# Batching half-array products and pulling a product ahead of its pair in a TensorE-bound mLSTM, Fourier-mix and MLP kernel

## The chip, the cores and the metric

The kernel runs on one core of a Trainium2 chip. Its time is the device time in microseconds (us). Runs of one kernel spread by about ±0.3 to ±0.5% (the kernel before: 420.44 to 422.69 us in the rounds of pair_only, 420.89 to 424.94 in those of best4), so differences below one per cent are given with a 95% interval from rounds (five for each experiment) in which the kernel in question and the kernel before ran on the same chip. A program on one core has no second die to be compared with; all runs used here count as fast. What does differ between runs is the mean clock granted to TensorE (0.991 to 1.000 in the runs of the changed kernel), which each run records, and which will matter.

In line numbers the kernel before and the changed one differ: L837 of the kernel before is L847 of the changed one (products of the first batch's MLP), L749 is L759, L897 is L907 (full-array products of the later MLPs), L902 is L912 (their 64-row products), L906 is L916 (adds), L772 is L782, L785 to L795 are L795 to L805, and the weight sum L971 is L998 (L988 in pair_only and pair_late). Lines up to L550 are the same in both.

## The reference, cut to what matters

```python
# four batches, 8 heads, 768 positions, head size 40
for t in range(S):                                  # attention, by decayed sums
    C = f_stab * C + i_stab * outer(v[t], k[t]); n = f_stab * n + i_stab * k[t]
    y[t] = sigmoid(o_gate[t]) * (C @ q[t]) / max(abs(n @ q[t]), 1)
x = heads side by side                              # 768 x 320
u = x + real(fft2(x))                               # Fourier mix
un = layernorm(u)
out = u + relu(un @ w_ch1) @ w_ch2                  # MLP, 320 -> 1280 -> 320
```

## The kernel before: the parts that matter

The kernel works through each batch in chunks of 128 positions. While TensorE does the MLP of one batch, the attention chunks of the next batch are woven in. Every piece of work is put into a plan under a slot and a phase, and emitted in that order:

```python
EVAC, FILL, MAIN, FILL_PE = range(4)          # phases within a slot
def at(slot, phase, fn, *args):
    plan.setdefault((slot, phase), []).append((fn, args))
```

An attention chunk has products of three shapes: the scores `ps` (L465) use half of the array's rows (40*128 in the trace, two at a time, 7 ns apart), the state product `ph<-qg,C` (L479) is full, and the chunk products `ph<-W,kvt` (L486) and `pc` (L496) use half of its columns (128*41 and 128*40, in pairs as well). The plan of a chunk, cut:

```python
def plan_mlstm(b, s0, stride=3):
    for c in range(NT):
        s = s0 + stride * c
        ...
        at(s - 1 if last else s, FILL_PE + (2.05 if last else 2), mlstm_scores, b, c)   # TensorE
        if b > 0:
            at(s + 1, FILL, mlstm_mask, b, c)                                           # GpSimd L443
        at(... s + 1, FILL + 0.1, mlstm_scale_q, b, c)                                  # GpSimd L431, qg
        at(s + 2, FILL, mlstm_decay, b, c)                                              # GpSimd L455
        at(... s + 2, FILL, mlstm_weigh, b, c)                                          # VectorE L471
        at(... s + 3, FILL_PE, mlstm_from_state, b, c)                                  # TensorE L479
        at(... s + 3, FILL_PE + 3, mlstm_from_chunk, b, c)                              # TensorE L486
        at(s + 3, FILL_PE + 3, mlstm_to_state, b, c)                                    # TensorE L496, VectorE L513/L515
        at(... s + 4, FILL, mlstm_gather, b, c)                                         # ScalarE L524, GpSimd L526
        ...
        at(x, FILL + 0.05, mlstm_finish, b, c)                                          # VectorE L544 to L550
```

The MLP has 320 = 128 + 64 + 128 features, so it too has products on half the rows (`tails`). From the second batch on, two groups of columns are multiplied by a scheme with sums in place of one of the products, one pair of hidden blocks at a time; `p1` is used four times, with copies and adds between:

```python
elif step == 2:
    product(p3, block(w1x["S4"], i), mlp_u(1, 2), True)
    product(p1, block(w1x["S3"], i), T3)
    nc.scalar.copy(out=h22, in_=p1)
else:
    tails(1, (p3, p5)); tails(0, (p2, p1))       # 64-row products
    product(p1, A[1, 1], T4)
    add(h12, p3); add(h22, p5); add(h11, p2)     # VectorE
    nc.scalar.activation(out=h21, in_=p1, func=AF.Relu, scale=-1.0)
```

During the first batch's MLP the weights, which come as 64-bit words, are unpacked on the side: `take` is two VectorE steps (L344, L346) that start a piece, `convert` is ScalarE's, `join` three more of VectorE (L358, L360, L364). And between an MLP's halves stands the inverse square root of the layer norm, four VectorE steps and twelve small GpSimd steps:

```python
when += [((s, 0.7), (s + 1, 0.7), (s + 2, 0.6)) for s in (33, 36, 39, 42, 45)]   # take, convert, join
...
at(s_mlp + NFF, FILL + 0.6, mix_rstd, b)
at((56, 57, 58, 72)[n], FILL + 0.4, out_weight_sums, n)                          # VectorE L971 (L988 in pair_only)
```

Of the kernel before, what the change touches and what calls it, by code (L numbers as in the profile page):

```python
# [19 lines left out]
L = 128  # L20
NT = S // L
# [5 lines left out]
NFF = DFF // L  # L27
TAIL = DM - 2 * L
TG = NT // 2
# [21 lines left out]
def kernel(  # L51
# [14 lines left out]
    nc = tc.nc  # L66
# [18 lines left out]
    def bank(name, shape, n=None):  # L85

        return ps_m.tile(shape, FP, name=name, tag=f"pm{next(turn) if n is None else n}")
# [16 lines left out]
    w1_sb = const.tile([L, 2, DFF], FP, name="w1_sb")  # L104
# [17 lines left out]
    def at(slot, phase, fn, *args):  # L122
        plan.setdefault((slot, phase), []).append((fn, args))
# [7 lines left out]
    EVAC, FILL, MAIN, FILL_PE = range(4)  # L131
# [405 lines left out]
    def mlstm_finish(b, c):  # L537

        k = chunks.pop((b, c))
        if c == 0:  # L540
# [9 lines left out]
        nc.vector.tensor_tensor(out=xs[b][:, c, 0:DM].rearrange("p (h d) -> p h d", d=D), in0=h1[:, :, 0:D], in1=sc,  # L550
                                op=OP.mult)

    def plan_mlstm(b, s0, stride=3):
        for c in range(NT):
            s = s0 + stride * c
            if b > 0:
                t = 22 + 2 * c if b == 1 and c < 3 else s - 5
                at(t, FILL, mlstm_load, b, c)
                at(t, FILL, mlstm_load_max, b, c)
                at(t, FILL, mlstm_load_decay, b, c)  # L560
                at(s, FILL, mlstm_load_o, b, c)
            if (b, c) > (0, 0):
                at(s, FILL, mlstm_exp, b, c, 0)
                at(s + 1, FILL - 0.5, mlstm_exp, b, c, NP)
                last = (b, c) == (0, NT - 1)
                at(s - 1 if last else s, FILL_PE + (2.05 if last else 2), mlstm_scores, b, c)
                if b > 0:
                    at(s + 1, FILL, mlstm_mask, b, c)
            at(s, FILL, mlstm_scale_v, b, c)
            at(s if (b, c) == (0, 2) else s + 1, FILL + 0.1, mlstm_scale_q, b, c)  # L570
            at(s + 2, FILL, mlstm_decay, b, c)
            end = (b, c) == (0, NT - 1)
            at(s + 1 if end else s + 2, FILL - 0.4 if end else FILL, mlstm_weigh, b, c)
            at(s + 2 if end else s + 3, FILL_PE, mlstm_from_state, b, c)
            at(s + 2 if end else s + 3, FILL_PE + (2 if end else 3), mlstm_from_chunk, b, c)
            at(s + 3, FILL_PE + 3, mlstm_to_state, b, c)
            at(s + 3 if end else s + 4, FILL, mlstm_gather, b, c)
            if b == 0:
                t, x = ((8, 11), (11, 14), (13, 14), (14, 15.5), (17, 18), (18, 21))[c]
            else:  # L580
                t = s + (8, 8, 7, 5, 5, 5)[c]
                x = t + 1
            at(t, FILL_PE + ((2.5 if c < 4 else 1) if b == 0 else 1), mlstm_turn, b, c, b == 0 and c < 4)
            at(x, FILL + 0.05, mlstm_finish, b, c)


# [259 lines left out]
    def hidden(gr, f):  # L846
        return hid[gr, f % 2][:, f // 2 * TG * L:(f // 2 + 1) * TG * L]  # L847
# [7 lines left out]
    def block(t, n):  # L855
        return t[:, n * L:(n + 1) * L]
# [20 lines left out]
    def mlp_u(gr, ch):  # L877
        return uT_bufs[gr][:, ch].rearrange("p c t -> p (c t)")
# [8 lines left out]
    def mlp_block(b, i, step):  # L887



        k = mixes[b]
        f = 2 * i
        T2, T3, T4 = w1x["T"]
        A = {(r, ch): block(w1_sb[:, ch], f + r) for r in range(2) for ch in range(2)}

        def product(bank, w, u, start=False):
            nc.tensor.matmul(bank, w, u, start=start, stop=True, skip_group_check=True)  # L897

        def tails(gr, banks):
            for r, bank in enumerate(banks):  # L900
                rows = slice(r * TAIL, (r + 1) * TAIL)
                nc.tensor.matmul(bank, block(w1t_sb, i)[rows], mlp_u(gr, 1)[rows], start=False, stop=True,  # L902
                                 skip_group_check=True)

        def add(h, bank):
            nc.vector.tensor_tensor(out=h, in0=h, in1=bank, op=OP.add)  # L906

        if step == 0:
            k.pm = [bank("pm", [L, TG * L], n) for n in (range(4) if i % 2 else range(3, -1, -1))]
        p1, p2, p5, p3 = k.pm  # L910
        (h11, h21), (h12, h22) = ([hidden(gr, f + r) for r in range(2)] for gr in range(2))
        if step == 0:  # L912
            product(p1, A[0, 0], mlp_u(0, 0), True)
            product(p2, A[0, 1], mlp_u(0, 2), True)
            nc.scalar.copy(out=h11, in_=p1)
        elif step == 1:  # L916
            product(p5, A[1, 0], mlp_u(1, 0), True)
            product(p1, block(w1x["S2"], i), T2)
            nc.scalar.copy(out=h12, in_=p1)  # L919
            add(h12, p5)  # L920
        elif step == 2:
            product(p3, block(w1x["S4"], i), mlp_u(1, 2), True)
            product(p1, block(w1x["S3"], i), T3)
            nc.scalar.copy(out=h22, in_=p1)
        else:
            tails(1, (p3, p5))
            tails(0, (p2, p1))
            product(p1, A[1, 1], T4)
            add(h12, p3)
            add(h22, p5)  # L930
            add(h11, p2)
            nc.scalar.activation(out=h21, in_=p1, func=AF.Relu, scale=-1.0)

    def mlp_relu_in_place(gr, f):
# [95 lines left out]
    def plan_mlp(b, s):  # L1030
        groups = range(NT // TG)
        for i in range(NFF // 2) if b > 0 else ():
            for step in range(4):
                at(s, MAIN, mlp_block, b, i, step)
                s += 1
            end = i == NFF // 2 - 1
            for n, (gr, f) in enumerate(((1, 2 * i + 1), (1, 2 * i), (0, 2 * i))):
                at(*((s, EVAC) if end else (s + n, MAIN + 0.5)), mlp_relu_in_place, gr, f)
        for gr in groups if b == 0 else ():
            for f in range(NFF):  # L1040
                at(s, MAIN, mlp_in, b, gr, f)
                s += 1
                if f % 2:
                    at(s, EVAC, mlp_relu, b, gr, f - 1)
                    at(s, EVAC, mlp_relu, b, gr, f)
        if b > 0:
            for j in range(1, 5):
                at(s - (5, 4, 3, 3)[j - 1], FILL_PE + 0.3, hidden_sums, 0, (j,), 0, NFF // 2 - 2)
            at(s, EVAC, hidden_sums, 0, (1, 2), NFF // 2 - 2, NFF // 2)
            at(s, MAIN + 0.1, hidden_sums, 0, (3, 4), NFF // 2 - 2, NFF // 2)  # L1050
        for n in range(TG) if b > 0 else ():
            for step in range(4):
                at(s, MAIN, mlp_out_pair, b, n, step)
                if n < TG - 1 and step > 1:
                    for j in (2 * step - 3, 2 * step - 2):
                        at(s, MAIN + 0.6, hidden_sums, n + 1, (j,))
                s += 1
        for gr in groups if b == 0 else ():
            for i in range(TG):
                for half in range(2):  # L1060
                    at(s, MAIN, mlp_out, b, gr, i, half)
                    s += 1
                at(s, EVAC, mlp_store, b, gr, i)
# [6 lines left out]
    def plan_batch(b, s_mlstm, s_mix, s_mlp):  # L1070
        plan_mlstm(b, s_mlstm)
        done = [s_mlstm + 3 * (j + NT // 2) + 7 for j in range(NT // 2)]
        assert s_mix >= done[-1] and s_mlp >= s_mix + 9
        late = [s_mlp + 2 * c for c in range(TG)]
        if b == 0:
            feat = [s_mix + 1, s_mix + 1, s_mlp + 3]
            turn = [s_mix + 2, s_mix + 3, s_mix + 4]
            add = turn + [s_mlp, s_mlp + 4, s_mlp + 6]
            late = [s_mlp + 2, s_mlp + 5, s_mlp + 7]
        else:  # L1080
            feat = [s_mix + c for c in ((3, 4, 6) if b == 1 else (3, 4, 7))]
            add = [s_mix + c for c in ((4, 4, 5, 6, 7, 7) if b == 1 else (4, 4, 5, 6, 8, 9))]
            turn = [s_mix + c for c in ((5, 6, 6) if b == 1 else (6, 7, 8))]
            late = [s_mix + c for c in ((7, 8, 8) if b == 1 else (9, 10, 10))]
            at(s_mlp, EVAC + 0.5, mlp_sums)
        plan_mix(b, s_mix, done, feat, add, turn + late)
        at(s_mlp + NFF, FILL + 0.6, mix_rstd, b)
        plan_mlp(b, s_mlp)
# [143 lines left out]
```

## Time and profile before

| kernel before | |
|---|---|
| time, median of the first three runs | 421.74 us (421.09 to 422.83) |
| span of the profiled run | 419.2 us |
| TensorE busy | 408.1 us, 97% |
| mean granted clock | 0.999 |

A reader should take three things from it. TensorE is the bound, so only its own stream counts. The stream has gaps of two kinds: small ones at each change of array shape (0.13 to 0.2 us each, with the late pass behind them; last section), and waits. And the waits are few; of the eleven lines in the view of TensorE's waits, these four are the ones to compare later (columns: what waited and for what; us in total, times, longest):

```profile
PE ph L479 <- DVE den L544: 0.6, 1, 0.6
PE po L999 <- DVE x L949: 0.6, 2, 0.3
PE pm L837 <- DVE x L749: 0.5, 1, 0.5
...
PE ph L479 <- POOL qg L431: 0.2, 1, 0.2
```

There is nearly nothing to be removed here. Everything that the change moves on VectorE and GpSimd must stay within that slack.

### The profile page before, as it was taken

To read this page: it belongs to the slowest core of one execution; us is meant where nothing else is said; L and a number is where in the kernel's file an instruction comes from. 1 tells how busy PE (TensorE), PEld (TensorE's weight loads), DVE (VectorE), ACT (ScalarE), POOL (GpSimd) and SP (SyncE) were. 2 spreads that over 40 slices of the span, in tenths; PEclk is the share of its full clock that TensorE was granted. 3 is DMA by queue.
4 is the path that set the end of the run, shared out by engine and by line. 5 is a ranking of instruction groups with operands and counts; after the bars stand their busy time and mean duration, and the time that the engine had idled before them with its cause. 6 is when DMAs were issued, how large, how long until landed. Compare 5 with 4: busy or idle time off the path is not lost.

```text
span 419.2 us, 8001 instructions
## 1 busy us (share of the span) xinstructions
PE 408.1 (97%) x2966; PEld 302.4 (72%) x2966; DVE 288.8 (69%) x682; ACT 189.5 (45%) x493; POOL 112.9 (27%) x194
## 2 busy tenths in 40 slices
PE   8999999999999999999999999999999999999997
PEld 6877555566567778776549998976559988455996
DVE  8789895777895638777765569788663786335652
ACT  6986376686561222654455413744451113355000
POOL 5554201468431520442231430351220000020000
PEclk9999999999999999999999999999999999999999
DMA  7899297567765254276100554310000000000010
GB/s 230 288 250 318 71 278 257 185 162 219 236 189 164 59 155 139 64 210 197 50 0 2 156 149 131 100 42 1 0 2 0 33 31 34 0 2 0 16 48 31
DMA packets 20549, 47.14 MB, mean 112 GB/s; under 512 B 2784, under 2 KB 9312, under 8 KB 20384
## 3 DMA queue, kind: packets, MB, share of 16 engines
q1 hardware_dynamic: 20512, 46.65, 36.7%
q8 instruction: 23, 0.38, 0.4%
q14 instruction: 14, 0.11, 0.1%
HBM read 42.52 MB, written 4.11 MB: 111 GB/s over the span
## 4 chain that ended last, share of the span: by engine, by line
PE 82%; DVE 7%; DMA 4%; issue 3%; ACT 2%; POOL 1%; ACTq 0%; DVEq 0%; POOLq 0%; SPq 0%
PE po L999 18%; PE pm L897 17%; PE po L943 8%; PE pm L902 5%; PE ps L465 5%; PE ph L486 4%; PE pu L729 4%; PE ph L479 3%; PE pm L837 3%; DMA raw<-in_w 3%; PE px L535 2%; PE put L772 2%; PE pz L698 2%; DMA kvt<-in_kv 1%; PE pz L686 1%
## 5 line engine op out<-in xcount | busy, mean ns | idle before, releaser
L949 DVE SCALAR_TENSOR_TENSOR x<-po,rstd,x 128x160 f32<-128x160 f32 (+1 forms) x69 | 27.0, 395 | 40.2 <-PE po L999 34.1
L906 DVE TENSOR_TENSOR h<-h,pm 128x384 f32<-128x384 f32 x60 | 30.5, 550 | 30.5 <-ACT h L919 20.9
L421 ACT ACTIVATE W<-W,colT 128x128 f32<-128x128 f32 x144 | 45.0, 395 | 0.0
L443 POOL TENSOR_SCALAR_AFFINE_SELECT W<-W 128x1024 f32<-128x1024 f32 x18 | 21.6, 1198 | 81.0 <-ACT W L421 59.1
L943 PE MATMUL po<-w_sb,h 128*128 128x320 f32 x120 | 34.4, 435 | 0.0
L897 PE MATMUL pm<-uT,w_sb 128*128 128x384 f32 x90 | 32.8, 492 | 0.2 <-DVE uT L885 0.2
L471 DVE TENSOR_TENSOR W<-ps,W 128x512 f32<-128x512 f32 x48 | 30.7, 680 | 2.6 <-POOL W L443 2.4
L837 PE MATMUL pm<-uT,w_sb 128*128 128x384 f32 x80 | 29.6, 499 | 0.7 <-DVE x L749 0.5
L777 ACT COPY uT<-put 128x384 f32<-128x384 f32 x24 | 11.2, 478 | 40.2 <-PE put L772 40.2
L943 PEld LDWEIGHTS po<-w_sb,h 128*128 128x128 f32 x120 | 22.2, 190 | 9.5 <-issue 0.8
L999 PE MATMUL po<-T,S 128*128 128x160 f32 x180 | 27.9, 302 | 0.6 <-DVE x L949 0.6
L465 PE MATMUL ps<-qk 40*128 40x128 f32 x384 | 27.8, 284 | 0.0
L999 PEld LDWEIGHTS po<-T,S 128*128 128x128 f32 x180 | 25.5, 190 | 2.2 <-DVE x L949 1.0
L792 POOL TENSOR_TENSOR t<-rstd 128x6 f32<-128x6 f32 x12 | 2.9, 244 | 89.2 <-DVE v L790 88.6
L999 PE MATMUL po<-w_sb,h 128*128 128x160 f32 x180 | 26.4, 301 | 0.0
L465 PEld LDWEIGHTS ps<-qk 40*128 40x128 f32 x384 | 23.4, 187 | 4.1 <-issue 0.7
L999 PEld LDWEIGHTS po<-w_sb,h 128*128 128x128 f32 x180 | 25.1, 190 | 1.3 <-DVE x L949 0.3
L486 PE MATMUL ph<-W,kvt 128*41 128x128 f32 x384 | 25.8, 277 | 0.0
L431 POOL TENSOR_TENSOR qg<-qk,Gb 128x512 f32<-128x512 f32 x18 | 25.2, 1402 | 0.1
L524 ACT COPY h<-ph 41x512 f32<-41x512 f32 (+1 forms) x16 | 9.3, 583 | 34.9 <-PE ph L486 34.8
L479 PEld LDWEIGHTS ph<-qg,C 128*128 128x128 f32 x160 | 20.0, 191 | 6.3 <-issue 2.5
L897 PEld LDWEIGHTS pm<-uT,w_sb 128*128 128x128 f32 x90 | 16.2, 190 | 10.8 <-DVE h L906 1.5
(207 smaller groups left out, 864.6 us busy)
## 6 DMA issues: line engine op xcount, KB each, us to landing
W<-M_d SPq DMA_DIRECT2D x18, 512.0 KB
kvt<-in_kv SPq DMA_DIRECT2D x24, 324.0 KB
qk<-in_qkT SPq DMA_DIRECT2D x48, 160.0 KB
raw<-in_w SPq DMA_DIRECT2D x10, 640.0 KB
Gb<-G_d SPq DMA_DIRECT2D x36, 128.0 KB
so<-in_o SPq DMA_DIRECT2D x24, 160.0 KB
out<-x SPq DMA_DIRECT2D x24, 160.0 KB
ds_sb<-in_dft_s SPq DMA_DIRECT2D x1, 1155.0 KB
```

Source lines behind the costliest of these rows:

```text
L421: nc.scalar.activation(out=k.W[:, h, :], in_=M, func=AF.Exp, scale=-1.0, bias=colT[:, c, 0, b * H + h:b * H + h + 1])
L431: nc.gpsimd.tensor_tensor(out=k.qg, in0=k.qk[:, 0], in1=k.Gb, op=OP.mult)
L465: nc.tensor.matmul(k.ps[hip][:, p, :], k.qk[r, 1, p, :], k.qk[r, 0, p, :], start=True, stop=True)
L471: nc.vector.tensor_tensor(out=Wv, in0=k.ps[hip], in1=Wv, op=OP.mult)
L479: nc.tensor.matmul(k.ph[:, p, :], k.C[:, p, :], k.qg[:, p, :], start=(p == 0), stop=False, skip_group_check=True)
L486: nc.tensor.matmul(k.ph[hip * 64:hip * 64 + D1, p, :], k.v1[:, 2 * p + hip, :], k.W[:, 2 * p + hip, :], start=(c == 0 and p == 0), stop=Tr ...
L837: nc.tensor.matmul(k.pm[i], w1_sb[:, ch, f0:f0 + L], u[2 * ch], start=(ch == 0), stop=False)
L897: nc.tensor.matmul(bank, w, u, start=start, stop=True, skip_group_check=True)
L906: nc.vector.tensor_tensor(out=h, in0=h, in1=bank, op=OP.add)
L943: nc.tensor.matmul(k.po, hidden(gr, f)[:, i * L:(i + 1) * L], w2_sb[:, f, :], start=(f == 0), stop=(f == NFF - 1))
L949: nc.vector.scalar_tensor_tensor(out=u, in0=po, scalar=k.rstd[:, c:c + 1], in1=u, op0=OP.mult, op1=OP.add)
L999: nc.tensor.matmul(po, a[:, f], w[:, f], start=start and f == 0, stop=f == half - 1, skip_group_check=True)
```

## The change

Its intent: (a) put chunk products with half rows or half columns next to the MLP's 64-row products, so that the array changes shape less often; (b) in the later MLPs, start the next pair's first product ahead of this pair's last, so that no product waits for ScalarE's copy; (c) issue the last ReLUs of a batch earlier. Cut to its core:

```diff
+    slots_of_halves = [s for s in range(32, 51, 2)] + [s for s0 in (65, 97) for s in range(s0, s0 + 17, 4)]
+    shifted = (35, 41, 68, 100)
+    def group(s):
+        return s + (s in shifted)
 ...
-  at(s - 1 if last else s, FILL_PE + (2.05 if last else 2), mlstm_scores, b, c)
+  at(s - 1 if last else group(s) if b > 0 else s, FILL_PE + (2.05 if last else 2), mlstm_scores, b, c)
 ...
+  g = group(s + 3) if b > 0 else s + 3
-  at(s + 2 if end else s + 3, FILL_PE, mlstm_from_state, b, c)
+  at(s + 2 if end else g, MAIN - 0.1 if b > 0 and g in slots_of_halves else FILL_PE, mlstm_from_state, b, c)
 ...                                       # chunk products, C: from s + 3 to g
-  at(s + 3 if end else s + 4, FILL, mlstm_gather, b, c)
+  at(s + 3 if end else g + 1, FILL + (0.05 if g > s + 3 else 0), mlstm_gather, b, c)
 ...                                       # px of the last chunk, and px in slots of halves: later
@@ mlp_block
+        def begin(i):                      # first product of pair i and its copy
+            k.p1 = bank("pm", [L, TG * L], 0 if i % 2 else 3)
+            product(k.p1, block(w1_sb[:, 0], 2 * i), mlp_u(0, 0), True)
+            nc.scalar.copy(out=hidden(0, 2 * i), in_=k.p1)
 ...
         elif step == 2:
             ...
+            tails(1, (p3, p5)); tails(0, (p2, p1))
+            add(h12, p3); add(h22, p5); add(h11, p2)
         else:
-            tails(1, (p3, p5)); tails(0, (p2, p1))
+            if i < NFF // 2 - 1:
+                begin(i + 1)
             product(p1, A[1, 1], T4)
-            add(h12, p3); add(h22, p5); add(h11, p2)
 ...
-  at(*((s, EVAC) if end else (s + n, MAIN + 0.5)), mlp_relu_in_place, gr, f)
+  at(*((s - 1, MAIN + (-0.1 if gr else 0.1)) if end else (s + n, MAIN + 0.5)), mlp_relu_in_place, gr, f)
```

## The prediction

> **What bounds the kernel now.** I read the page first, then the waits of TensorE, then TensorE's timeline in the four MLP stages, and last VectorE's timeline where the change leans on it. From the page:
>
> ```profile
> span 419.2 us, 8001 instructions
> PE 408.1 (97%) x2966; PEld 302.4 (72%) x2966; DVE 288.8 (69%) x682; ACT 189.5 (45%) x493; POOL 112.9 (27%) x194
> PE 82%; DVE 7%; DMA 4%; issue 3%; ACT 2%; POOL 1%; ACTq 0%; DVEq 0%; POOLq 0%; SPq 0%
> ```
>
> TensorE is the bound: busy 97% of the span and 82% of the chain that ended last. No engine beside it has much to say on average, so a gain can come only from TensorE's own stream: fewer products, or the same products closer together. The change removes no product. What can be closer is visible in the last batch's MLP, where nothing else runs. Columns are start and length in us:
>
> ```profile
> 363.24 0.81 PE L897 MATMUL pm<-uT,raw 128*128 128x384 f32 x2
> 363.97 0.91 PE L897 MATMUL pm<-e,raw 128*128 128x384 f32 x2
> 364.81 1.56 PE L902 MATMUL pm<-uT,w1t_sb 64*128 64x384 f32 x8
> 366.30 0.91 PE L897 MATMUL pm<-m,w_sb 128*128 128x384 f32 x2
> 367.05 2.10 PE L897 MATMUL pm<-uT,w_sb 128*128 128x384 f32 x6
> 368.99 0.81 PE L897 MATMUL pm<-raw 128*128 128x384 f32 x2
> ```
>
> Read the differences of starts, not the lengths. Six plain passes take 367.05 to 368.99, 0.323 us each (an f32 product is two passes). The 64-row products run two at a time, so their eight passes should take 4 x 0.323 = 1.29 us; they take 1.49. The product after them takes 0.75 instead of 0.65. The one before takes 0.84, of which 0.10 follows a wait (below) and 0.09 comes with the change of shape. So full array to half rows and back costs 0.09 + 0.20 + 0.10 = 0.4 us, about 0.2 us a switch: part of it the gap at the switch, part of it a late second pass. Half rows to half columns is cheaper (0.13 us by the same reckoning at 187 to 189 us).
>
> The second loss is in the first two lines: 363.24 to 363.97 is 0.73 us where two passes need 0.65. The product L923 accumulates into the bank that ScalarE's copy is still reading (the copy ends at 363.91). With the late second pass this costs 0.19 us, and it recurs in 11 of the 15 pair blocks.
>
> [...]
>
> **The change part by part.**
>
> (1) Batching. I counted the shapes in the built orders: 148 switches before, 134 after. Five chunks in the first batch's MLP lose two each (full, rows, columns, full, rows, full becomes full, rows, columns, full); two places in each of the second and third batches' MLPs lose one each. 14 x 0.2 = 2.8 us off TensorE's stream. All of it lies on the path, if the moved products find their inputs.
>
> (2) Pair order. For every pair but the first, L918's product now comes ahead of L917's, so two products (1.29 us) stand between it and L923's instead of one. ScalarE's copy (0.48 us) then fits. 10 of the 11 waits go: 10 x 0.19 = 1.9 us. The eleventh, pair 0 of the last batch, keeps the old order.
>
> (3) The next pair's first product now follows the 64-row products at once. Its bank is the one that VectorE's first add (L929) frees. In the last MLP the first add starts 0.95 us after the 64-row products start and takes about 0.55, and TensorE would be ready after 1.49: so about 0.1 us of new wait, at 6 places where no chunk product lies between: +0.6 us.
>
> (4) The last Relus of a batch are issued before the last product. In the last batch the first sum of hidden blocks waits for the third of them (388.16, sum at 388.19), and TensorE stands 0.31 us at 389.1 because of it. Once the second add is done, at about 386.0, four ScalarE operations at a pitch of 0.45 us end at 387.9: -0.3 us.
>
> Without new waits that is -2.8 - 1.9 + 0.6 - 0.3 = -4.4 us, 417.3. I don't believe it, because of three places where a state product (L479) or an add now stands behind VectorE.
>
> (5) First batch's MLP, the chunk at 99 us:
>
> ```profile
> 93.72 0.68 DVE L515 TENSOR_TENSOR C<-C,pc 40x164 f32<-40x164 f32 x2
> 96.46 0.50 DVE L344 TENSOR_SCALAR e<-raw 128x640 uint32<-128x640 uint32 x1 [2.07 <-DMA raw<-in_w]
> 96.89 1.37 DVE L346 TENSOR_SCALAR m<-raw 128x640 uint32<-128x640 uint32 x1
> 98.29 1.29 DVE L471 TENSOR_TENSOR W<-ps,W 128x512 f32<-128x512 f32 x2
> 99.44 1.16 PE L479 MATMUL ph<-qg,C 128*128 128x128 f32 x8 [0.23 <-POOL qg L431]
> ```
>
> In the new order the state update C comes after the two L344/L346 steps and L471. It can't start before the weights have landed (96.46, some 0.6 us earlier after what was saved by then), so it ends at 99.7; but the state product now stands ahead of a full product and its 64-row pair, and TensorE is free for it at about 96.6. A wait of 3.1 us replaces one of 0.23. An earlier state product (80.18 us) gets about 0.7 us in the same way, VectorE having a mask multiply (1.29 us) ahead of the copies. Against it, the wait of 0.5 us at 76.58 nearly goes, since VectorE's adds no longer stand behind the copies (-0.5 by my placing), and the later wait of 0.61 us at 110.2 is swallowed by the lag (-0.75 with its late pass). The stage: -2.0 (10 switches) - 0.5 + 0.7 + 2.9 - 0.75 = +0.4 us.
>
> (6) Second batch's MLP. Pair 0: the state product moves ahead of two products, to 184.7, but its bank is freed by L550 at 185.08: +0.6 with the late pass. Pair 2: the transpose px moves from ahead of the pair's first products to behind them, and with it a chain on VectorE:
>
> ```profile
> 200.98 0.17 DVE L544 TENSOR_SCALAR den<-px 128x8 f32<-128x8 f32 x1 [0.45 <-PE px L535]
> ...
> 202.55 0.98 DVE L971 TENSOR_TENSOR w_sb<-w_sb 128x800 f32<-128x800 f32 x1
> 204.07 0.56 DVE L906 TENSOR_TENSOR h<-h,pm 128x384 f32<-128x384 f32 x1 [0.54 <-ACT h L919]
> 204.54 0.49 DVE L606 TENSOR_TENSOR eo<-x 128x320 f32<-128x320 f32 x1
> ...
> 206.13 0.16 DVE L785 TENSOR_SCALAR v<-x 128x6 f32<-128x6 f32 x1
> ...
> 206.69 1.48 DVE L906 TENSOR_TENSOR h<-h,pm 128x384 f32<-128x384 f32 x3
> ```
>
> From the end of px: normalizing 1.65, L971 0.95, add 0.55, fold 1.65, L785 and its three followers 0.6, first add 0.55 = 6.0 us until the bank is free. TensorE has from there four products (2.58), the switch and the 64-row products (1.49): 4.1 us. So 1.9 us of wait, split between the 64-row product of the bank being added and the next pair's first product. Stage: -0.4 - 0.6 (three waits of part 2) - 0.2 (a wait of this chain that is there now at 206.9) + 0.6 + 1.9 + 0.3 (small ones) = +1.6 us.
>
> (7) Third batch's MLP: no L971, so 0.9 instead of 1.9; but L550 ends at 279.45 while the state product would be ready at 278.2: 1.4 against 0.14 now. -0.4 - 0.6 - 0.4 + 1.5 + 0.9 + 0.1 = +1.1 us.
>
> (8) Last batch: -0.8 (four waits) - 0.3 + 0.4 = -0.7 us. Sum +0.4 + 1.6 + 1.1 - 0.7 = +2.4 us, 424.1.
>
> **Rivals.** First, the intended one: VectorE and GpSimd move up with TensorE, the transfers too, and the waits of (5) to (7) shrink: 417 to 419. For it: only some slots are shifted (35, 41, 68, 100, but not 47), which looks like a choice made by trial; and 40 us of VectorE idle lie in other places. Against it: the transfer's issue at 90.28 waits for GpSimd, and the VectorE chains are made of durations, not gaps. Second, that a new wait of 3 us drops the clock (PEclk is 9 all along[...]): some us more, 427 or so. Third, that all is given back in the output stages, where TensorE waits little (0.6 us on L949 in all): then no change.
>
> **Range and chances.** The working says 424.1. I trust its signs more than its sizes, and give the first rival a quarter of the weight: 423.2. Eight times in ten 418.0 to 427.0. 2% is 8.4 us; neither account reaches it. Faster 0.02, same 0.95, slower 0.03.
>
> **What would show it.** Right: 14 fewer switches; no wait of L923's successor on ScalarE after pair 0; in the first MLP a wait of 2 to 3 us of a state product near 97 us on VectorE; in the second and third MLP waits of 1 to 2 us of the pair's first product on L906's successor. The MLP stages of batches two and three longer, the last shorter by 0.5 to 1 us. Wrong: if the state product near 97 us waits under 1 us, (5) falls; if the pair-2 waits stay under 0.5 us, (6) and (7) fall, and the time is below 420.

## The result

The changed kernel took 426.62 us (median of 4 runs, 424.6 to 427.8) beside 422.03 us of the kernel before (4 runs, 421.09 to 422.83). The ratio is 1.0105, 95% interval 1.0056 to 1.0153. A ratio here is the mean time of a kernel's fast runs over that of the other's fast runs in the same rounds, so it is not quite the ratio of the two medians. By the 2% rule the two are the same; the interval says that the changed one is slower by about 1%. Outputs are correct.

The page of the changed kernel:

```profile
span 424.1 us, 8013 instructions
PE 406.3 (96%) x2966; PEld 305.0 (72%) x2966; DVE 288.6 (68%) x682; ACT 189.0 (45%) x493; POOL 113.4 (27%) x194
PE 73%; DVE 15%; DMA 5%; issue 4%; ACT 3%; POOL 1%; DVEq 0%; ACTq 0%; POOLq 0%
```

Compare with the page lines in the prediction: TensorE is busy for 1.8 us less, and the span is 4.9 us longer. VectorE's share of the chain that ended last went from 7% to 15%. So something now stands still that did not, and VectorE is named. The changed kernel's waits of TensorE, same columns as before:

```profile
PE ph L479 <- DVE C L515: 2.8, 1, 2.8
PE pm L847 <- DVE x L759: 2.1, 1, 2.1
PE pm L907 <- DVE h L916: 1.9, 2, 1.1
PE ph L479 <- DVE x L550: 1.6, 2, 1.3
```

These are 8.4 us of waits where the list before had 1.9 (the lines left out sum to 5.6 us before and 5.9 after). To see where the time comes in, I matched the products of the two traces: the k-th execution of a product's line in one with the k-th in the other, and took the difference of their starts, the offset. The first output product of the first batch, for instance, starts at 122.60 in one trace and at 126.14 in the other: offset 3.54. Offsets are constant where nothing changed (3.54 from there to 180 us, 4.83 from 221 to 273, 5.87 from 315 to 353), so what each stage added is the difference of two constants:

| stage (times of the kernel before) | predicted by the working | added in the trace |
|---|---|---|
| start, to 57 us | 0 | +0.34 |
| first batch's MLP, 57 to 122 | +0.4 | +3.20 |
| second, 181 to 220 | +1.6 | +1.28 |
| third, 274 to 314 | +1.1 | +1.05 |
| last, 354 to 388 | -0.7 | -0.95 |
| span | +2.4 | +4.9 |

Three of the four stages came out within 0.35 us. The first MLP is the surplus, and within it the part up to 84 us (two chunks): it added 2.51 us there, and only 0.69 more up to the end. Here is that place in the kernel before, first VectorE, then GpSimd (start, length, what):

```profile
74.31 0.50 DVE L344 TENSOR_SCALAR e<-raw 128x640 uint32<-128x640 uint32 x1
74.72 0.49 DVE L346 TENSOR_SCALAR m<-raw 128x640 uint32<-128x640 uint32 x1
...
75.95 0.49 DVE L749 TENSOR_TENSOR x<-x,pu 128x320 f32<-128x320 f32 x1
```

```profile
74.53 0.33 POOL L526 COPY h_first<-h 128x4 f32<-128x4 f32 x1 [8.91 <-ACT h L524]
74.81 1.35 POOL L443 TENSOR_SCALAR_AFFINE_SELECT W<-W 128x1024 f32<-128x1024 f32 x1
```

and in the changed kernel, all engines in one:

```profile
73.81 1.35 POOL L443 TENSOR_SCALAR_AFFINE_SELECT W<-W 128x1024 f32<-128x1024 f32 x1 [7.85 <-ACT W L421]
74.24 1.27 DVE L344 TENSOR_SCALAR e<-raw 128x640 uint32<-128x640 uint32 x1
...
75.13 1.50 POOL L431 TENSOR_TENSOR qg<-qk,Gb 128x512 f32<-128x512 f32 x1
...
75.43 1.55 DVE L346 TENSOR_SCALAR m<-raw 128x640 uint32<-128x640 uint32 x1
...
77.60 0.49 DVE L759 TENSOR_TENSOR x<-x,pu 128x320 f32<-128x320 f32 x1
...
78.24 3.76 PE L847 MATMUL pm<-uT,w_sb 128*128 128x384 f32 x6 [2.08 <-DVE x L759]
```

Before, GpSimd waited for the gathered row (L526) until 74.5 and did its mask behind it. The change moves the gather one slot on, so GpSimd is free earlier, and its mask (L443) and q scaling (L431) lie beside VectorE's L344 and L346. Those two take 1.27 and 1.55 us instead of 0.50 and 0.49, the adds behind them come 1.65 us later, and TensorE, whose next bank is the one that L759 reads, stands for 2.08 us. That GpSimd beside them is the cause is tested by a run below (mask_late).

The lines say more: it is not any overlap that costs; the long times are those in which GpSimd started first. In the kernel before, L346 also lay beside the mask, but had started first (74.72 against 74.81) and kept its 0.49 us. In the changed kernel GpSimd started first both times, and each VectorE step ended 0.35 us after GpSimd's instruction (75.51 after 75.16, 76.98 after 76.63), as if held until that was over. In the traces of the kernel before and the changed one, L344 and L346 took more than 0.52 us 13 times, and in all 13 they ended 0.35 us (to 0.01) after a GpSimd instruction that had started before them; in the four cases in which the mask (L443) or the gather (L526) started only while they ran, they took 0.49 to 0.50 us. (One L346, at 106.69 in the kernel before, took 0.48 us inside an L443 that the trace has at 5.88 us.)

The second thing to see is the 3.76 us: six products' passes that take 2.1 us elsewhere. The same stretch by microseconds (the ninth number, after POOL's, is the granted clock):

```profile
77.00:78.00 1.00, 0.00 (x0) 0.00 (x0) 0.93 (x3) 0.99 (x4) 0.00 (x0) 1.00 0.95 338
78.00:79.00 1.00, 0.76 (x1) 0.50 (x2) 0.93 (x4) 0.97 (x3) 0.19 (x1) 0.52 0.64 164
79.00:80.00 1.00, 1.00 (x3) 0.68 (x2) 1.00 (x3) 1.00 (x2) 0.00 (x0) 0.50 1.25 137
80.00:81.00 1.00, 1.00 (x3) 0.40 (x2) 0.94 (x4) 1.00 (x4) 0.59 (x2) 0.50 0.64 147
81.00:82.00 1.00, 1.00 (x5) 0.62 (x4) 1.00 (x2) 1.00 (x3) 0.92 (x2) 0.77 0.97 371
```

After the wait TensorE works at half clock, for 0.96 + 1 + 1 + 0.46 = 3.42 us (a mean of 0.52 over a microsecond is 0.96 us at half), which costs at most half of that, 1.71 us. (The last section shows what in the traces goes with the drop: not the wait's length alone, but where it falls.) Of the four runs of the changed kernel, one kept the full clock and is the fastest (1.000, 424.6 us); two have a mean clock of 0.996, which is one such stretch (1.71 of 424), and one has 0.991, about two stretches.

The 2.79 us wait at 100 us was predicted. These are GpSimd's lines there and then VectorE's, in the changed kernel:

```profile
99.17 0.20 POOL L805 TENSOR_TENSOR rstd<-t,rstd 128x6 f32<-128x6 f32 x1
99.32 1.37 POOL L443 TENSOR_SCALAR_AFFINE_SELECT W<-W 128x1024 f32<-128x1024 f32 x1
```

```profile
99.24 0.49 DVE L344 TENSOR_SCALAR e<-raw 128x640 uint32<-128x640 uint32 x1 [2.58 <-DMA raw<-in_w]
...
100.95 1.27 DVE L471 TENSOR_TENSOR W<-ps,W 128x512 f32<-128x512 f32 x2
102.15 0.67 DVE L515 TENSOR_TENSOR C<-C,pc 40x164 f32<-40x164 f32 x2
```

VectorE stands 2.58 us for the weights' DMA with the C sums queued behind: their products (L496) end at 97.61, and L515, behind L344, L346 and L471 in the plan, starts at 102.15. But look at GpSimd: its mask, on which L471 depends, starts at 99.32, because the twelve small steps of the inverse square root stood ahead of it. Two causes end within 0.1 us of each other, and only one is named.

### The profile page after: what moved, and what is told of

Its sections match the earlier page's. It is cut to its first block, busy times and chain, and to the rows that moved or that the text cites. A ratio compares the mean times of both kernels' runs of the same rounds, so it can differ in the third digit from the quotient of the medians.

```text
span 424.1 us, 8013 instructions
## 1 busy us (share of the span) xinstructions
PE 406.3 (96%) x2966; PEld 305.0 (72%) x2966; DVE 288.6 (68%) x682; ACT 189.0 (45%) x493; POOL 113.4 (27%) x194
## 4 chain that ended last, share of the span: by engine, by line
PE 73%; DVE 15%; DMA 5%; issue 4%; ACT 3%; POOL 1%; DVEq 0%; ACTq 0%; POOLq 0%
PE po L1026 17%; PE pm L907 14%; PE po L970 8%; PE pm L912 5%; PE ps L465 4%; PE ph L486 4%; DMA raw<-in_w 3%; PE ph L479 3%; PE pu L739 3%; PE pm L847 2%; PE px L535 2%; DVE W L471 2%; PE pz L708 2%; DMA kvt<-in_kv 1%; PE pz L696 1%
## 5 line engine op out<-in xcount | busy, mean ns | idle before, releaser
L916 DVE TENSOR_TENSOR h<-h,pm 128x384 f32<-128x384 f32 x60 | 30.5, 549 | 31.8 <-PE pm L907 16.0
L443 POOL TENSOR_SCALAR_AFFINE_SELECT W<-W 128x1024 f32<-128x1024 f32 x18 | 21.3, 1185 | 93.8 <-ACT W L421 70.1
L907 PE MATMUL pm<-uT,w_sb 128*128 128x384 f32 x90 | 37.5, 503 | 2.1 <-DVE h L916 1.9
L847 PE MATMUL pm<-uT,w_sb 128*128 128x384 f32 x80 | 31.3, 520 | 2.5 <-DVE x L759 2.1
L471 DVE TENSOR_TENSOR W<-ps,W 128x512 f32<-128x512 f32 x48 | 30.7, 680 | 3.7 <-POOL W L443 3.4
L479 PE MATMUL ph<-qg,C 128*128 128x128 f32 x160 | 21.5, 277 | 5.2 <-DVE C L515 2.8
L431 POOL TENSOR_TENSOR qg<-qk,Gb 128x512 f32<-128x512 f32 x18 | 25.1, 1393 | 0.7 <-DMA Gb<-G_d 0.6
```

The lines of the kernel that those rows point to most:

```text
L431: nc.gpsimd.tensor_tensor(out=k.qg, in0=k.qk[:, 0], in1=k.Gb, op=OP.mult)
L471: nc.vector.tensor_tensor(out=Wv, in0=k.ps[hip], in1=Wv, op=OP.mult)
L479: nc.tensor.matmul(k.ph[:, p, :], k.C[:, p, :], k.qg[:, p, :], start=(p == 0), stop=False, skip_group_check=True)
L847: nc.tensor.matmul(k.pm[i], w1_sb[:, ch, f0:f0 + L], u[2 * ch], start=(ch == 0), stop=False)
L907: nc.tensor.matmul(bank, w, u, start=start, stop=True, skip_group_check=True)
L916: nc.vector.tensor_tensor(out=h, in0=h, in1=bank, op=OP.add)
```

## The experiments

My theory: the switches saved are real (14 x 0.2 us), and the loss is work on VectorE and GpSimd that came to stand ahead of or beside what TensorE waits for, plus the half clock that follows a long wait (2.08 us in the changed kernel's profile). The rivals: the saving isn't there at all; the pair order, not the batching, does the damage; the waits have other causes and only move when one is removed. Growth of the offset by stage is read as above. Here is all of it in one table; the texts draw on it (us added, from the profiled run of each):

| run | time, us (runs) | ratio, 95% interval | first MLP | second | third | last |
|---|---|---|---|---|---|---|
| changed kernel | 426.62 (4) | 1.0105, 1.0056 to 1.0153 | +3.20 | +1.28 | +1.05 | -0.95 |
| pair_only | 421.71 (6) | 0.9999, 0.9982 to 1.0017 | +0.67 | +0.94 | +0.36 | -0.95 |
| batch_only | 427.38 (6) | 1.0129, 1.0104 to 1.0153 | +3.41 | +1.15 | +1.10 | 0.00 |
| no35 | 424.41 (6) | 1.0063, 1.0042 to 1.0083 | +2.87 | +1.29 | +1.05 | -0.96 |
| no41 | 424.95 (6) | 1.0069, 1.0048 to 1.0090 | +2.38 | +1.29 | +1.06 | -0.95 |
| take_late | 422.77 (6) | 1.0018, 0.9999 to 1.0037 | +0.50 | +1.28 | +1.04 | -0.97 |
| mask_late | 429.02 (6) | 1.0170, 1.0142 to 1.0198 | +6.44 | +1.27 | +1.05 | -0.97 |
| state_back | 427.33 (6) | 1.0124, 1.0096 to 1.0153 | +3.73 | +2.14 | +1.44 | -0.97 |
| pair_late | 419.53 (6) | 0.9936, 0.9916 to 0.9957 | +0.80 | -0.41 | -0.21 | -0.97 |
| before_late | 420.81 (6) | 0.9963, 0.9934 to 0.9992 | +1.31 | -0.22 | -0.22 | 0.00 |
| best2 | 418.93 (6) | 0.9914, 0.9886 to 0.9942 | -1.92 | -0.18 | +0.50 | -0.95 |
| best3 | 416.71 (5) | 0.9861, 0.9837 to 0.9886 | -2.18 | -0.61 | -0.40 | -0.96 |
| best4 | 415.58 (5) | 0.9828, 0.9798 to 0.9857 | -3.94 | -0.60 | -0.41 | -0.95 |

The ratio of a row is to the kernel before in the same rounds; its median there was between 421.58 and 422.89 us. All runs gave correct outputs.

### pair_only: the pair order and the ReLUs alone

The edit is the change in `mlp_block` and of the ReLU line, with the plan of the chunks as before.

> Only the order inside the pairs and the last ReLUs' places; no batching. My theory: this half of the change is a gain wherever it is at work, and the loss is all the batching's. The last batch's MLP, where nothing is batched, became 0.95 us shorter from the kernel before to the changed one (offset 5.87 to 4.92 us); three MLPs of this kind give 2.8 us, so 419 us, ratio about 0.993, and the first batch's part (up to 181 us) unchanged to 0.1 us. Rival: the new order costs VectorE waits in the second and third MLP where attention work shares VectorE, and gives back what it gains in the last: 421 to 422 us, ratio 0.998 to 1.0, offsets in the second and third MLP at or above zero.

Measured: 421.71 us, no gain. The rival was right. The last MLP gains its 0.95 us, the second and third lose 0.94 and 0.36. (The +0.67 of the first MLP is no effect: TensorE's order there is the old one, and 0.59 of it is one DMA that landed later in this execution, with L344 and the wait on L544 behind it.) The losses are two waits of the new first product, which the old order did not have, of 1.06 us at 209 us and 0.55 us at 303. VectorE's queue ahead of the first:

```profile
207.57 0.33 DVE L613 TENSOR_TENSOR fe<-eo 128x159 f32<-128x159 f32 x1
207.81 0.17 DVE L785 TENSOR_SCALAR v<-x 128x6 f32<-128x6 f32 x1
...
208.36 1.48 DVE L906 TENSOR_TENSOR h<-h,pm 128x384 f32<-128x384 f32 x3
```

TensorE's product comes at 208.96, when the first of the three adds has freed its bank. From the start of the 64-row products to this product it is 2.91 us, and 2.11 in the third MLP, where the kernel before has 1.49: so 1.42 and 0.62 us lost, part of it inside the 64-row products. Before these lines stand a fold (L606 to L613) and a weight sum of 0.98 us (L988). So the wait that I had put down to the moved transpose px is there without that move: it is the pair order that leaves less slack, and VectorE's queue that uses it up.

### batch_only: the batches alone

The edit is the change in `plan_mlstm`, with `mlp_block` and the ReLUs as before.

> Only the three batches, with the order inside the pairs as before. My theory: the first batch's MLP loses 3.2 us as in the changed kernel (it has no pairs), and the second and third, without the gain of the pair order, lose more than the 1.3 and 1.0 us they lose now, some 2 us each: 427 to 429.5 us, ratio 1.013 to 1.018. Rival: the second and third MLP lose only because pair order and batching collide in pair 2 (the first add waits behind the px group); then with the old order the batching gives its switches there (0.5 to 0.8 us each faster) and the total is about 424 us, ratio 1.005.

Measured: 427.38 us. The first MLP loses as in the changed kernel, as expected. The second and third lose 1.15 and 1.10, half of the 2 us that I expected, though the rival's gain isn't there either. With the pair order they lose 1.28 and 1.05, so on top of the batches it costs next to nothing, while alone it cost 0.94 and 0.36; the two don't add, and I did not separate why. Its six runs fall in two groups: three with a mean clock of 1.000 took 425.37 to 426.78, three with 0.992 (two half-clock stretches by the reckoning above) 427.98 to 428.29, some 2 us apart. The same kernel thus has the half clock in some executions and not in others.

### no35 and no41: one shift taken out

```diff
-    shifted = (35, 41, 68, 100)
+    shifted = (41, 68, 100)        # no35
+    shifted = (35, 68, 100)        # no41
```

> The changed kernel with slot 35 left out of the shifted ones: scores of that chunk and state product of the one before are at their old place in the first batch's MLP. My theory: the 2.08 us wait of the first product on x (L759) at 76 us comes from the weight conversion steps of VectorE (L344, L346), which now run beside GpSimd's mask and take 1.3 and 1.6 instead of 0.5 us, ahead of L759, and the halved clock after it from the wait: both go, at a cost of one or two switches. Offset against the kernel before by the put of 83.7 us falls from 2.85 to about 0.5 us, the total by 2 to 2.5 us to about 424.3 us, ratio 1.005, TensorE clock of 1.00 at 78 to 82 us. Rival: the wait comes from something else in the batching (scores now at MAIN - 0.1, C copies), and stays at 1 us or more with clock 0.5.

> The changed kernel with slot 41 left out of the shifted ones. My theory: the 2.79 us wait of the state product on C at 100 us goes, since the copies of C (L515) then stand ahead of L344 and L346 again, which wait for a DMA; 2.8 us less 0.6 for switches and for the shorter wait at 110 us that it swallowed (0.75): about 1.5 us less than the changed kernel, 425 us, with the 2.08 us wait at 76 us still there. Rival: the DMA arrives late whatever the order, the wait moves to the next product on x (L759) or to W (L471), and the total stays at 426 to 427 us.

Measured: without the shift at slot 35 the wait on L759 is 0.5 us, as in the kernel before, the clock stays full there, and the part up to 84 us adds 0.76 instead of 2.51 us. The time is 424.41 us, as expected. In the profiled execution the gain of the whole is only 0.3 us, since the half clock now comes at 102 us, behind the wait on C, which stays at 2.6 us: one long wait removed, and the half clock follows the other one. Four of the six runs have such a clock (mean 0.995 or 0.996); two kept 1.000. Without the shift at 41 the wait on C is gone, but the same state product waits 1.6 us for GpSimd's q scaling (L431) instead. The time fell by 1.7 us, as expected, and the rival was right that another cause stood close behind; it only named the wrong one.

### take_late: the conversion steps moved, the products left

```diff
-  when += [((s, 0.7), (s + 1, 0.7), (s + 2, 0.6)) for s in (33, 36, 39, 42, 45)]
+  when += [((s + 1, 0.06) if s in (36, 42) else (s, 0.7), (s + 1, 0.7), (s + 2, 0.6)) for s in (33, 36, 39, 42, 45)]
```

> The changed kernel, every product in its place; two pieces of the weight conversion have their first two VectorE steps (L344, L346) later: one behind the steps on x (L753 to L759), the attention sums and the first C copies, one behind the C sums (L515). My theory: both long waits of the first batch's MLP (2.08 us at 76 us, 2.79 us at 100 us) and with them the halved clock go, and what is left is the saving of ten shape switches: offset against the kernel before at 122.7 us from +3.5 to between -2 and -0.5 us, the total 4 to 5 us less than the changed kernel, 421 to 422.5 us, ratio 0.999 to 1.003, clock 1.00 in every run. Rival: TensorE waits for something else there (the DMA of the weights, GpSimd's qg, ScalarE's ReLUs), and the offset stays above +1.5 us and the ratio above 1.006.

Measured: 422.77 us, some 4 us less than the changed kernel, with TensorE's order unchanged. The wait at 76 us is gone altogether, and the part up to 84 us now saves 1.27 us. But half of my expectation failed: with the DMA out of the way, the state product still waits 2.26 us for C. VectorE's and GpSimd's lines in this run:

```profile
96.71 1.29 DVE L471 TENSOR_TENSOR W<-ps,W 128x512 f32<-128x512 f32 x2 [3.76 <-POOL W L443]
```

```profile
95.44 0.20 POOL L805 TENSOR_TENSOR rstd<-t,rstd 128x6 f32<-128x6 f32 x1
95.59 1.09 POOL L443 TENSOR_SCALAR_AFFINE_SELECT W<-W 128x1024 f32<-128x1024 f32 x1
```

L471 waits for the mask, and the mask for the inverse square root chain ahead of it. That is the second cause seen above; the DMA had covered it. Three of its six runs have one half-clock stretch (mean clock 0.996), which is behind this wait in the profiled one.

### mask_late: GpSimd's mask apart from the conversion steps

```diff
-  at(s + 1, FILL, mlstm_mask, b, c)
+  at(*((s + 2, FILL + 0.06) if (b, s) == (1, 35) else (s + 1, FILL)), mlstm_mask, b, c)
   # and mlstm_scale_q of the same chunk to (s + 2, FILL + 0.07)
```

> The changed kernel with one mask and one q scaling of GpSimd (L443, L431) behind GpSimd's copy of the gathered row (L526), where the kernel before had them. My theory: GpSimd came free earlier, since that copy had moved behind them, and its work then lay beside VectorE's L344 and L346; with them apart again L344 and L346 take 0.5 us each (now 1.27 and 1.55), the wait for L759 at 76 us falls from 2.08 to about 0.3 us, and the clock stays full there; but the mask is now at 78 us or later, so a wait of up to 1.5 us on the sums with W (L471) may follow, and the 2.8 us wait on C at 100 us stays and may now be what halves the clock: 424 to 425.5 us. Rival: L344 and L346 are slow for another reason (the DMA that writes into the same memory): they stay above 1 us, and so does the wait.

Measured: L344 and L346 take 0.50 and 0.49 us with nothing of GpSimd beside them, and the wait on L759 is gone (0.15 us is left):

```profile
72.56 0.50 DVE L344 TENSOR_SCALAR e<-raw 128x640 uint32<-128x640 uint32 x1
72.97 0.49 DVE L346 TENSOR_SCALAR m<-raw 128x640 uint32<-128x640 uint32 x1
```

So GpSimd's work beside them was the cause of their slowness, and the rival about the DMA falls. As a version it is the worst of all, well above the 424 to 425.5 us expected: the mask and the q scaling now come at 77 and 78 us, the state product waits 3.26 us for L431, and the half clock lasts 6.82 us, twice 3.41. By their mean clock (0.987 to 0.992) all six runs have two such stretches or three.

### state_back: the state product behind the 64-row products again

```diff
-  MAIN - 0.1 if b > 0 and g in slots_of_halves else FILL_PE
+  MAIN - 0.1 if b == 1 and g in slots_of_halves else FILL_PE
```

> The changed kernel with the state product of the third and fourth batches' attention (in the second and third MLP) back behind the 64-row tails. My theory: the waits of the state product on VectorE (L550; 0.38 and 1.27 us) go, two switches of 0.2 us come at each of two places, so 0.85 us less than the changed kernel in all, the second MLP the same to 0.2 us and the third shorter by 0.8 us; the waits on L916 at pair 2 stay. Rival: VectorE is late by then whatever the place of the product, the wait moves to the scores (for their bank) or to the next product, and nothing is gained or 0.8 us is lost.

Measured: the two waits on L550 are gone, as expected, and the second and third MLP are nevertheless longer by 0.86 and 0.39 us than in the changed kernel. The rival was right. The trace has three more changes of shape in each of the two MLPs, some 0.6 us by my figure. And in each of the two MLPs the 64-row products at one place take 2.45 us from first start to last end instead of 1.56 (at a second place of the third MLP 1.96); the trace puts the late ones down to VectorE's adds (L916), so in the changed kernel the state product, ahead of them, had given that add its time. So the early state product with its wait is better than the late one without. I didn't try to split the 0.86 further.

### pair_late and before_late: VectorE's queue ahead of the adds

```diff
-  at(s_mlp + NFF, FILL + 0.6, mix_rstd, b)
+  at(s_mlp + NFF + 2, FILL + 0.6, mix_rstd, b)
-  at((56, 57, 58, 72)[n], FILL + 0.4, out_weight_sums, n)
+  at((56, 57, 58, 76)[n], FILL + 0.4, out_weight_sums, n)
```

pair_late has these two moves on top of pair_only, before_late on the kernel before.

> The pair order alone, with the rstd chain (L785 to L790) and one weight sum (L988) of VectorE moved behind the three adds of that pair, on which the next pair's first product waits in the new order. My theory: the waits of 1.06 and 0.55 us on L906 come from VectorE's queue ahead of the adds (0.65 us rstd chain, 0.98 us weight sum); they fall below 0.3 us in all, so the second and third MLP become 0.1 to 0.3 us faster than in the kernel before instead of 0.95 and 0.36 us slower, and the total is 420.3 us, ratio 0.997. Rival: the fold steps (L606 to L618, 1.7 us) and the finish of the chunk are enough to keep the adds late, 0.5 us or more of the waits stay, and the ratio is 0.999.

> The kernel before with only the two moves of the fourth run of the last call: the rstd chain (L785 to L790 on VectorE, twelve small GpSimd steps L792 to L795 behind it) two slots later, one weight sum (L988) four slots later. My theory: the old order did not wait there (no wait on L906 of 0.1 us or more in its profile), so this alone gains at most the 0.1 us of switches around pair 2 and stays at the time of before, ratio 0.998 to 1.001; then the 0.6 per cent of the fourth run belong to the pair order, freed of its two waits. Rival: the moves gain by themselves (GpSimd's mask and q scaling come earlier), ratio 0.995 or less, and the pair order is worth little.

Measured: in pair_late no wait on the adds of 0.1 us is left, and it is faster than the kernel before, ratio 0.9936. The moves alone give 0.9963, more than I expected: the rival had a part of the truth. The second and third MLP gain 0.22 us each by the moves alone, and the wait of 0.23 us for GpSimd's q scaling near 99 us is gone. The pair order's own share is then about 0.9936 / 0.9963 = 0.9973, some 1.1 us. The two intervals together leave about 0.0036 on either side, so the times alone don't show it; the traces do, with 0.97 us less in the last MLP. (The +1.31 of before_late's first MLP holds two DMA waits of its profiled execution, 0.77 us on qk and 0.59 more than usual on a weight piece near 107 us; the six runs show a gain.)

### best2, best3, best4: the whole change with its waits taken out

best2 is the changed kernel with the edits of take_late and pair_late. best3 moves the state product of two places within the batch:

```diff
-  MAIN - 0.1 if b > 0 and g in slots_of_halves else FILL_PE
+  FILL_PE + 2.5 if g in (65, 97) else MAIN - 0.1 if b > 0 and g in slots_of_halves else FILL_PE
```

best4 is best3 with `s in (36, 42, 45)` for the late conversion steps.

> The whole change, with the two conversion steps moved (as in take_late) and the rstd chain and the weight sum moved (as in pair_late); products of TensorE in the changed kernel's order. My theory: the 2.26 us wait on C that stayed at 98.7 us was GpSimd's rstd chain ahead of the mask (L443) on which the sums with W (L471) and, behind them in order, the C sums wait; with it gone the first batch's MLP shows the switch saving, offset at 122.7 us from +0.9 to -1.5 to -2.5 us; second and third MLP without the waits of 1.06 and 0.82 us on L916 are at -0.2 to +0.6 us each; last -0.95. Total 417 to 418.5 us, ratio 0.989 to 0.992, clock 1.00. Rival: another wait of 1 us or more takes its place at 98 us (qg L431 or a DMA), and the ratio is 0.995 or more, no better than the pair order alone with the late chain (0.9936).

> As best2, with the state product of the first pairs of the second and third MLP between the scores and the chunk products (still one batch: tails, scores, state, chunk products, the same number of switches) instead of ahead of the tails. My theory: the waits of 0.38 and 1.27 us on L550 go, 1.2 to 1.6 us less than best2, about 416.3 us, ratio 0.987. Rival: as with the state product moved back behind the tails, what it covered comes out elsewhere (tails or scores wait for ScalarE's copies or VectorE), and it is within 0.5 us of best2.

> As best3, with the first two conversion steps of one more weight piece (its L344 waited 2.0 us for its DMA at 104 us, with the sums with W and the finish of a chunk behind it in VectorE's queue) behind the steps on x. TensorE's order is the same. My theory: a DMA that comes when it comes stood ahead of work that TensorE waits for; the wait of the state product of 1.1 to 1.4 us at 109 us (0.6 to 1.2 us in the kernels before it too) goes, 0.8 to 1.2 us less than best3, about 415.8 us, ratio 0.984, and the spread of the runs becomes smaller. Rival: the sums with W wait for GpSimd's mask or for their scores, and the wait stays or moves to the next state product: 416.7 us as best3.

Measured: best2 takes 418.93 us, a little more than I expected (the ratio is inside). The wait on C at 98 us is gone, the clock is 1.000 in all runs, and the first MLP saves 1.92 us. best3 takes 416.71 us: the waits on L550 go, and all four MLPs are shorter than before. The expectation was wrong about the switches: the full-array state product now splits half rows from half columns, one change of shape more at each of the two places (134 in the trace against 132 in best2's). best4 takes 415.58 us, ratio 0.9828: the wait at 109 us behind a late DMA, which the kernel before has too, is gone. It is faster than the kernel before by 1.7%, and its interval reaches past 2%. Not all of that is the change's: before_late shows 0.4% from the two moves, and the late conversion steps were not tried on the kernel before by themselves. My estimate is that they could take away at most its waits of 0.52 (L749) and 0.61 us (L544) there, some 0.3%, which leaves about 1% for the change.

## Why the prediction was right, and where it was wrong

The predicted time was 423.2 us, the range 418.0 to 427.0, the class "within 2%". The measured 426.62 lies in the range, but by 0.4 us, and two of the four runs (427.43 and 427.80) lie above it: that the median fell inside is partly luck. By its own steps:

- **(1) Batching removes 14 switches.** Right. Counting the changes of shape between products in the traces gives 146 before and 132 after (some records are missing, so two fewer than in the program). That they are worth 0.2 us each shows only when the waits are gone: best3's first MLP, with ten fewer, is 2.18 us shorter, though that sum also holds a wait of 0.5 us that left (L749) and one behind a DMA that was 0.5 us longer.
- **(2) Pair order.** The waits went as said: of 11 late starts of L923's product (0.41 us after its forerunner instead of 0.32) one is left, that of pair 0 in the last batch. With (3) and (4) it was to gain 1.6 us; freed of its own waits it gains about 1.1 (the traces of pair_late and before_late).
- **(3) New wait on the first add.** Right, and smaller: the next product starts 1.55 instead of 1.49 us after the 64-row products at six places, 0.36 us in all where 0.6 was predicted. (The prediction's own figures, 0.95 + 0.55 against 1.49, give 0.01 a place; it wrote 0.1.)
- **(4) and (8) Last batch.** Predicted -0.7, measured -0.95.
- **(6) and (7).** Predicted +1.6 and +1.1, measured +1.28 and +1.05. The waits named are there. On the adds the prediction split its wait between the 64-row products and the pair's first product: together they lose 1.79 and 0.89 us (3.28 and 2.38 us instead of 1.49; predicted 1.9 and 0.9), of which the first product's own waits are 1.06 and 0.82. The state product waits for L550 0.38 and 1.26 us (predicted 0.6 and about 1.4, with the late pass). The sizes were right, but the reason given for the adds was wrong in part. pair_only loses 1.42 and 0.62 without px moved, so px and the rest of the batching added 0.37 and 0.27; the rest is the pair order with the rstd chain, the weight sum and the fold ahead of the adds, and pair_late removes it.
- **(5) First batch's MLP.** This is the term that failed: +0.4 predicted, +3.20 measured. The wait of the state product was sized well (3.1 predicted, 2.79 measured), though its cause was half seen: not only the DMA but, within 0.1 us of it, the chain on GpSimd. What failed is the item "the wait of 0.5 us at 76.58 nearly goes (-0.5 by my placing)". It grew to 2.08 us. I had placed VectorE's steps with the durations of the old profile, L344 and L346 at 0.5 us, and had not asked what GpSimd would do once its gather moved. The old profile had the answer: the prediction itself quotes L346 at 1.37 us, at 96.89, beside the mask. In the terms of the sum: -2.0 for the switches, +1.56 (2.08 less the old 0.52) where -0.5 was predicted, +2.56 for the state product (2.9), nothing at 80 us (+0.7), -0.61 at 110 us (-0.75), and at most 1.71 for the half clock, which the sum did not have, make +3.2.
- **Second rival, the clock.** It was a guess: the trace of the kernel before has the full clock from 5.64 to 418.65 us and shows no drop behind a wait within the run. I gave it no weight of its own, and it came true in most executions: three of the changed kernel's four have a mean clock of 0.991 or 0.996. The one run of the changed kernel at full clock took 424.6 us, and the others 1.2 to 3.2 us more. That 424.6 is next to the working's 424.1 does not confirm (5): without the half clock the first MLP would still be about 1.5 us longer or more (3.20 - 1.71), where +0.4 was predicted.
- **First rival, everything moves up together.** It was to have a quarter of the weight, which moved the figure the wrong way. (The sum is off too: a quarter on 417 to 419 gives about 422.6; 423.2 is a weight of some 15%.) It became true only when the work in the way was moved by hand.

Where did the expected gain go? It is there, in TensorE's busy time (1.8 us less) and in best2 to best4. In the change as it stood it was paid back in four kinds of wait, all of them for engines that are not the bound: L344 and L346 held up by GpSimd's mask and q scaling, C behind a DMA and the rstd chain, the adds behind that chain and a weight sum, the state product's bank behind L550. The half clock came on top.

## What to carry to other kernels

When the bound engine's stream is made denser, what feeds it on the other engines loses slack (four lines of waits went from 1.9 to 8.4 us here), and a step that moves later on one of them lets the next one start earlier: ask for each moved item what now runs in its old place, and beside what. Count a wait's possible causes, not the one that ends it: here two ended within 0.1 us of each other, and removing the named one alone left 2.26 of 2.79 us. And keep instructions that wait for a DMA behind those that the bound engine needs (VectorE stood 2.58 us for one here, with the C sums behind it); moving the first steps of three weight pieces, the rstd chain, a weight sum and a state product at two places turned a 1% loss into a 1.7% gain.

## What the traces show of the hardware

- The clock. Waits of 2.08 us (changed kernel) and 2.26 us (take_late) were followed by a half clock, while batch_only's profile, with waits of 2.1 and 2.6 us, kept its clock. The half-clock stretches within a run (its first microseconds and its end left out) lasted 3.41 to 3.42 us (five profiles) or 6.82 (mask_late). In the two traces compared above the changes of the clock lie 71.680 and then 3.413 us apart (changed kernel) and 413.013 us apart (kernel before), which is 21, 1 and 121 times 3.413. So I divided these two traces into stretches of 3.413 us, counted from the first change, and added up TensorE's idle time in each, from 20 us on (by the profile's modelled ends). In the changed kernel the stretch that ends at 78.04 us holds 1.87 us of it and is followed by the half clock; the next two, with 1.75 (up to 101.93) and 1.73 us, are not, nor is any other. In the kernel before one stretch holds 2.51 us, the one that ends at 418.65, where the clock drops; no other has more than 0.84. In the five other profiles that have a half clock, the 3.41 us ahead of it hold 2.0 to 2.5 us of idle time, by rows of a microsecond. Length alone does not decide: the changed kernel's longest wait, 2.79 us at 100 us, is split by a border into 1.75 and 1.03 us, and the clock stayed. That executions without a profile differ for the same reason is likely and not shown. (Of 42 runs of the kernel before beside the experiments, two had a mean clock of 0.996, at 424.2 and 424.9 us; none of them was profiled.)
- Weight loads beside products: in the last MLP of the kernel before, full-array weight loads of 0.19 us start 1 to 2 ns after full-array products (367.051 after 367.050 us), and the products keep their pitch of 0.323 us.
- VectorE beside GpSimd: L344 and L346 (128x640, one SBUF input) took 0.49 us alone and 1.27 to 1.55 in the changed kernel's two places beside L443 or L431, always ending 0.35 us after GpSimd's instruction, and the small GpSimd steps of the rstd chain 0.66 to 0.81 us beside VectorE's two-input steps and 0.20 to 0.24 alone. L743 of the kernel before, which reads PSUM, kept its 0.32 us beside L443.
- A change of shape cost about 0.2 us between full and half rows (kernel before, 363.97 to 366.73 us), of which half is a late second pass of the next f32 product (0.427 us after the first instead of 0.323), and 0.13 between half rows and half columns (187.84 to 188.19 us).
